# An identity matrix made on VectorE instead of GpSimd, and a first block's products in another order

## The chip, the cores and the metric

The kernel runs on one core of a Trainium2 chip. Its engines work side by side, each through its own list of instructions: TensorE (matrix products; PE in the profile, its weight loads PEld), VectorE (DVE), ScalarE (ACT), GpSimd (POOL) and SyncE (SP, which here only issues transfers). An engine waits on semaphores that others raise. Transfers (DMA) are issued from the queues of SP, ACT and POOL and run on 16 DMA engines. The metric is the device time of one execution in microseconds. It was 277.08 us before the change, the median of three runs (276.8 to 277.09).

## The reference

A dense layer, a GELU, a second dense layer, and the gradients of everything. Inputs are in bf16: x (1, 2048, 448), w1 (448, 1792), b1, w2 (1792, 448), b2 and grad_out, here g, in x's shape.

```python
def _gelu(x):
    return jax.nn.gelu(x, approximate=True)

def _fwd_reference(x, w1, b1, w2, b2):
    h = jnp.einsum("bsd,df->bsf", x, w1) + b1
    h = _gelu(h)
    return jnp.einsum("bsf,fd->bsd", h, w2) + b2

def reference(x, w1, b1, w2, b2, grad_out):
    _out, _vjp = jax.vjp(_f, x, w1, b1, w2, b2)
    _grads = _vjp(grad_out)
    return (_out0, *[jnp.asarray(_g) for _g in _grads])
```

So there are six outputs: the layer's output and the gradients of x, w1, b1, w2 and b2.

## The kernel before

All work is written in one order by hand; each engine takes its instructions in that order, and waits are put in where data or buffers ask for them. Hidden features lie on the partitions: a step g handles two tiles of 128 features (h = 0, 1) for one block of 512 rows. There are four blocks of seven steps, 28 steps in all. The first block begins with row 512, since `row0(b)` turns the blocks by one.

In a step, TensorE makes u = w1ᵀ xᵀ (`M1`, L243, and its last 64 of 448 rows in `rest`, L253) and q = w2 gᵀ (`M4`, L262, and `rest`, L256). ScalarE takes u out of PSUM with the bias (L288), squares it (L289), makes the GELU (L290) and a tanh (L382). VectorE builds the argument of the tanh (L379), the GELU's slope (L386 to L389) and multiplies it with q (`dve_gate`, L393). The two results, h and gh, are weights for the pieces of the output and of x's gradient (`Unit.piece`, L424). After the 28 steps come the last block's pieces, the gradient of w1 (L590, L598) and that of w2 (L609).

x, g and w2 come transposed by DMA on SP's queue (`load_x`, `load_g`, `load_w2T`), w1 and w2 plain; all early loads but three are issued from SP in one row, those three from ACT. g's first block is loaded in two halves of 256 rows.

The start differs from the other steps (step 0 is `first_products`, `turn_w2`, `first_chain`):
- VectorE clears four small tiles (L188 to L191). One is `warm`, which TensorE multiplies eight times (`keep_warm`, L282) before data is there.
- `make_identity`, a library helper (masks.py), makes a 128 x 128 identity in bf16, `ident`, in a part of the tile T that step 1 uses later: a memset on GpSimd (masks.py:197) and an affine select (masks.py:199).
- b1 comes as 14 rows of 128; VectorE turns it into a column for each tile with four 32 x 32 transposes (L484) and a cast (L485). The bias is first used by L325 on ScalarE and L326 on VectorE.
- `first_products` makes u of step 0, once for each half of the block's rows (L299, L302).
- `turn_w2` turns w2's first 256 rows on TensorE (the transposed loads bring the other rows): eight products of w2 (as weights) with `ident` (L313) into two PSUM tiles. `turned(0)` and `turned(1)` copy them to w2T on ScalarE (L317).
- `M1(1)` and `rest(1, None)` make u of step 1 (L243, L253).
- `first_chain` runs the GELU of step 0 in halves on ScalarE and VectorE, and then `first_q`: q of step 0 for each half r of g's rows, first with the row tiles 0 and 1 of g, then with 2 and the 64 rows that are left (L276). Between the two parts stand four products of the output (L424). `gate(0)` and `gate(1)` (L349) multiply the halves into gh.

Of the kernel before, what the change touches and what calls it, by code (L numbers as in the profile page):

```python
# [8 lines left out]

ACT = mybir.ActivationFunctionType  # L10
ALU = mybir.AluOpType
BF16 = mybir.dt.bfloat16
F32 = mybir.dt.float32
# [6 lines left out]
def kernel(  # L20
# [15 lines left out]
    nc = tc.nc  # L36
    P = 128
# [6 lines left out]
    KF = KD - 1  # L44
    DL = D - KF * P
    DOV = D - P
    DM = KF * P
    SB = 512
# [20 lines left out]
    psum_h = first.enter_context(tc.tile_pool(name="psum_h", bufs=1, space=bass.MemoryType.PSUM))  # L69
# [17 lines left out]
    T_flat = const.tile([P, 4 * 2 * SB], BF16, name="T")  # L87
# [5 lines left out]
    w2T_sb = w2T_flat.rearrange("p (k f) -> p k f", k=KD)  # L93
# [12 lines left out]
    def gq(b):  # L106
        o = ((b % 2) * 2 + 1) * KD * SB
        return xg_flat[:, o:o + KD * SB].rearrange("p (k s) -> p k s", k=KD)
# [5 lines left out]
    def hT(g):  # L114
        return ring(hT_flat, HR, g)

    def ghT(g):
        return ring(ghT_flat, GR, g)

    def V_of(g):  # L120
        return VA_flat[:, 0:2 * SB].rearrange("p (h s) -> p h s", h=2)

    def A_of(g):
        return VA_flat[:, 2 * SB:4 * SB].rearrange("p (h s) -> p h s", h=2)

    def B_of(g):
        return ring(B_flat, 1, g)

    def t_of(g):
        return ring(T_flat, 4, 2 * (g % 2))  # L130

    def p_of(g):
        return ring(T_flat, 4, 2 * (g % 2) + 1)
# [8 lines left out]
    HB = SB // 2  # L142
# [7 lines left out]
    def load_x(b, r0=0, r1=SB):  # L150
        src = x2[row0(b) + r0:row0(b) + r1, :]
        dst = xq(b)[:, :, r0:r1]
        if row0(b) > 0:
            turn_in(dst, src, DL - P)
        else:
            nc.sync.dma_start_transpose(out=dst[:, 0, :], in_=src[:, 0:P])
            nc.sync.dma_start_transpose(out=dst[:, 1:KD, :], in_=src[:, DL:D])
            nc.gpsimd.tensor_copy(out=dst[DL:P, 0, :], in_=dst[0:DL, 0, :])
# [30 lines left out]
    nc.vector.memset(ones, 1.0)  # L189
    nc.vector.memset(b1_rows, 0.0)  # L190
    nc.vector.memset(w128[:], 1.0 / P)  # L191
    ident = T_flat[:, 6 * SB:6 * SB + P]
    make_identity(nc, ident)
    load_x(0, 0, HB)
    load_x(0, HB, SB)
    nc.scalar.dma_start(out=w1_sb[:, 1:KD, 0:256], in_=w1[DL:D, 0:256].rearrange("(k p) f -> p k f", p=P))
# [28 lines left out]
    def blk(g):  # L225
        return divmod(g, NPAIR)

    def cols(g, h):
        c = g % NPAIR
        return slice((2 * c + h) * P, (2 * c + h + 1) * P)  # L230

    u_of = {}
    g_of = {}
# [28 lines left out]
                nc.tensor.matmul(g_of[g][:, h, :], lhsT=w2T_sb[:, kt, cols(g, h)], rhs=gq(g // NPAIR)[:, kt, :],  # L262
                                 start=False, stop=(kt == KF - 1), skip_group_check=True)

    def first_q(kts):


        for r in range(2):
            rs = slice(r * HB, (r + 1) * HB)
            if kts[0] == 0:  # L270
                g_of.setdefault(0, []).append(psum_h.tile([P, SB], F32, name="h%d" % r))
            q = g_of[0][r]
            for kt in kts:
                ps = slice(0, DL if kt == KF else P)
                for h in range(2):
                    nc.tensor.matmul(q[:, h * HB:(h + 1) * HB], lhsT=w2T_sb[ps, kt, cols(0, h)], rhs=gq(0)[ps, kt, rs],  # L276
                                     start=(kt == 0 and h == 0), stop=(kt == KF),
                                     tile_position=(0, 0) if kt == KF else None, skip_group_check=True)

    def keep_warm(n, weights, moving):  # L280
        for i in range(n):
# [34 lines left out]
    def turned(i):  # L316
        nc.scalar.copy(out=w2T_sb[:, 2 * i:2 * i + 2, 0:2 * P], in_=(ta, pw)[i].rearrange("p (k f) -> p k f", k=2))  # L317

    def first_chain():

        V, A, Bt, t, p, h0 = V_of(0), A_of(0), B_of(0), t_of(0), p_of(0), hT(0)
        R = (slice(0, HB), slice(HB, SB))

        def copy(r):
            nc.scalar.activation(out=V[:, 0, R[r]], in_=u_of[0][r][0], func=ACT.Identity, bias=b1_col[:, 0:1])  # L325
            nc.vector.tensor_scalar(out=V[:, 1, R[r]], in0=u_of[0][r][1], scalar1=b1_col[:, 1:2], scalar2=None,  # L326
                                    op0=ALU.add)

        def square(r):
            nc.scalar.activation(out=A[:, :, R[r]], in_=V[:, :, R[r]], func=ACT.Square,  # L330
                                 scale=math.sqrt(3.0 * GELU_C * GELU_A))

        def gelu(r):
            nc.scalar.activation(out=h0[:, :, R[r]], in_=V[:, :, R[r]], func=ACT.Gelu_apprx_tanh)

        def tanh(r):
            nc.scalar.activation(out=t[:, :, R[r]], in_=Bt[:, :, R[r]], func=ACT.Tanh, scale=-1.0 / 3.0)

        def cubic(r):
            nc.vector.scalar_tensor_tensor(out=Bt[:, :, R[r]], in0=A[:, :, R[r]], scalar=3.0 * GELU_C, in1=V[:, :, R[r]],  # L340
                                           op0=ALU.add, op1=ALU.mult)

        def slope(r):
            nc.vector.scalar_tensor_tensor(out=p[:, :, R[r]], in0=A[:, :, R[r]], scalar=GELU_C, in1=h0[:, :, R[r]],
                                           op0=ALU.add, op1=ALU.mult)
            nc.vector.tensor_scalar(out=p[:, :, R[r]], in0=p[:, :, R[r]], scalar1=-0.5, scalar2=None, op0=ALU.add)

        def gate(r):
            nc.vector.scalar_tensor_tensor(out=ghT(0)[:, :, R[r]], in0=t[:, :, R[r]], scalar=1.0,  # L349
                                           in1=g_of[0][r].rearrange("p (h s) -> p h s", h=2), op0=ALU.add, op1=ALU.mult)  # L350

        def times(r):
            nc.vector.tensor_scalar(out=t[:, :, R[r]], in0=t[:, :, R[r]], scalar1=1.0, scalar2=None, op0=ALU.add)
            nc.vector.tensor_tensor(out=t[:, :, R[r]], in0=t[:, :, R[r]], in1=p[:, :, R[r]], op=ALU.mult)

        copy(0)
        square(0)
        gelu(0)
        cubic(0)
        copy(1)  # L360
        turned(0)
        square(1)
        tanh(0)
        gelu(1)
        turned(1)
        slope(0)
        cubic(1)
        tanh(1)
        times(0)
        slope(1)  # L370
        times(1)
        first_q((0, 1))
        run_pieces([U["o", 0, j] for j in (0, 0, 1, 1)])
        first_q((2, KF))
        gate(0)
        gate(1)

# [70 lines left out]
    def run_pieces(units):  # L448
        for un in units:
            if un.piece():  # L450
                full.append(un)
# [7 lines left out]
    U = {(k, b, j): Unit(k, b, j) for k in "og" for b in range(NB) for j in range(SPB)}  # L459
# [28 lines left out]
    M1(1)  # L488
    rest(1, None)
    first_chain()  # L490
    first.close()
    psum_g = ctx.enter_context(tc.tile_pool(name="psum_g", bufs=1, space=bass.MemoryType.PSUM))
    for g in range(NSTEP):
        b, c = blk(g)
        pieces = [U[k] for k in seq[b] for _ in range(NF)]
        n = len(pieces)
# [84 lines left out]
    for t0, t1 in ((0, 4), (4, HT)):  # L581
        n = (t1 - t0) * P
        for h in range(2):
            a0, a1 = t0 + h * HT, t1 + h * HT
            cs = slice(a0 * P, a1 * P)
            for kt in range(KF):
                ps = psum_a.tile([P, SB], F32, name="acc")
                psv = ps[:, 0:n].rearrange("p (t f) -> p t f", f=P)
                for st in range(NS):
                    nc.tensor.matmul(psv, lhsT=x_all[:, st, kt * P:(kt + 1) * P], rhs=gh_rows(st, a0, a1),  # L590
                                     start=(st == 0), stop=(st == NS - 1))
                nc.scalar.copy(out=gw1_all[:, kt, cs], in_=ps[:, 0:n])  # L592
            nc.scalar.dma_start(out=out_2[0:KF * P, cs].rearrange("(k p) f -> p k f", p=P), in_=gw1_all[:, :, cs])
        ps = psum_a.tile([P, SB], F32, name="acc")
        for st in range(NS):
            for h in range(2):
                psv = ps[h * DL:(h + 1) * DL, 0:n].rearrange("p (t f) -> p t f", f=P)
                nc.tensor.matmul(psv, lhsT=x_all[:, st, KF * P:D], rhs=gh_rows(st, t0 + h * HT, t1 + h * HT),  # L598
                                 start=(st == 0), stop=(st == NS - 1), tile_position=(0, h * DL), skip_group_check=True)
        nc.scalar.copy(out=gw1_rem[:, t0 * P:t1 * P], in_=ps[:, 0:n])  # L600
        for h in range(2):
            nc.scalar.dma_start(out=out_2[KF * P:D, (t0 + h * HT) * P:(t1 + h * HT) * P],
                                in_=gw1_rem[h * DL:(h + 1) * DL, t0 * P:t1 * P])


    for ft in range(NF):
        ps = psum_a.tile([P, SB], F32, name="acc")
# [41 lines left out]
```

## Time and profile before

| | |
|---|---|
| time, median of three runs | 277.08 us |
| the profiled execution's own time | 276.89 us |
| its span, first to last instruction | 275.1 us |
| granted TensorE clock | 1.000 |
| TensorE busy | 266.6 us, 97% of the span |
| VectorE busy | 191.0 us, 69% |
| ScalarE busy | 145.2 us, 53% |
| GpSimd busy | 54.4 us, 20% |
| TensorE in the first 7.30 us / from 7.30 to 9.20 us | 5.81 / 0.06 us busy |
| VectorE from 14.8 to 40.0 us | 24.10 of 25.20 us busy |

The profile is of one execution. Times in it count from the first instruction. A line number stands for the source line that made an instruction; where a library made it, its file is named. Tiles are called by the names of the buffers they lie in: `w_x` holds w1, `w_gw` w2, `w2T_g` w2 transposed, `xg_h` the turned x and g, `T` several small tiles, `ident` among them. An instruction of a sequencer (a register move, a semaphore, a configuration, a DMA issue) is not counted as busy. "Landing" is the time from a DMA's issue to its last semaphore update.

### The profile page before, as it was taken

How to read it: one execution, taken by the hardware profiler on the slowest of the kernel's cores; microseconds unless marked ns; L12 is line 12 of the kernel's file. 1: busy time of each engine (PE TensorE's matmuls, PEld its weight loads, DVE VectorE, ACT ScalarE, POOL GpSimd, SP SyncE). 2: the span in 40 equal slices, each digit the busy share in tenths (PEclk: the TensorE clock that was granted, in tenths of full speed). 3: DMA queues.
4: the chain of work that ended last, by engine and by line, in shares of the span. 5: the costliest groups of instructions: out<-in, count | busy, mean ns of one | idle time of the engine just before them, and what ended most of it. 6: DMA issues, size and time to landing. Idle time of an engine off the chain costs nothing.

```text
span 275.1 us, 3612 instructions
## 1 busy us (share of the span) xinstructions
PE 266.6 (97%) x1397; PEld 124.8 (45%) x1411; DVE 191.0 (69%) x229; ACT 145.2 (53%) x193; POOL 54.4 (20%) x61
## 2 busy tenths in 40 slices
PE   7799999999999999999999999999999999999995
PEld 3343434344344434444444445554445655555552
DVE  2799999999999999999988871149999960000000
ACT  3787888788888878887677750021111211112111
POOL 0000000850211503032030236111700039200000
DMA  7999899999589956245634329999989931101111
GB/s 163 210 270 218 154 218 173 210 328 163 120 204 193 265 69 134 52 132 122 161 110 79 111 80 217 314 343 252 182 170 308 209 101 57 38 15 50 52 49 34
DMA packets 100477, 43.52 MB, mean 158 GB/s; under 512 B 89036, under 2 KB 97100, under 8 KB 100460
## 3 DMA queue, kind: packets, MB, share of 16 engines
q1 hardware_dynamic: 93376, 26.65, 51.0%
q0 software_dynamic: 4512, 14.69, 17.2%
q10 hardware_dynamic: 2572, 1.95, 2.3%
q8 instruction: 11, 0.18, 0.3%
q14 instruction: 6, 0.05, 0.1%
HBM read 7.00 MB, written 14.23 MB: 77 GB/s over the span
## 4 chain that ended last, share of the span: by engine, by line
PE 85%; DVE 9%; issue 4%; ACT 1%; POOL 0%; DVEq 0%; POOLq 0%
PE acc L424 28%; PE acc L609 15%; PE acc L590 13%; PE q L262 11%; PE u L243 10%; PE u L253 4%; PE acc L598 2%; DVE ghT_h L393 2%; DVE T L386 2%; DVE Bt L379 2%; DVE T L389 1%; PE h L276 1%; DVE T L387 1%; DVE T L388 1%; PE q L256 0%
## 5 line engine op out<-in xcount | busy, mean ns | idle before, releaser
L424 PE MATMUL acc<-w_gw,hT_h 128*128 128x448 bf16 x224 | 46.5, 352 | 0.0
L424 PE MATMUL acc<-w1T_gw,ghT_h 128*128 128x448 bf16 x224 | 45.1, 352 | 0.0
L288 ACT ACTIVATE VA<-u,b_col 128x512 f32<-128x512 f32 x54 | 34.0, 681 | 13.3 <-PE u L253 13.3
L262 PE MATMUL q<-xg_h,w2T_g 128*128 128x512 bf16 x161 | 39.4, 381 | 0.2 <-issue 0.2
L243 PE MATMUL u<-xg_h,w_x 128*128 128x512 bf16 x149 | 38.4, 379 | 1.2 <-ACT VA L288 0.6
L393 DVE SCALAR_TENSOR_TENSOR ghT_h<-T,q 128x1024 bf16<-128x1024 bf16 x27 | 33.0, 1221 | 8.3 <-PE q L262 6.6
L590 PE MATMUL acc<-gh_nat,w_x 128*128 128x512 bf16 (+1 forms) x192 | 36.7, 353 | 0.0
L382 ACT ACTIVATE T<-Bt 128x1024 bf16<-128x1024 f32 x27 | 28.5, 1057 | 14.0 <-DVE Bt L379 13.9
L386 DVE SCALAR_TENSOR_TENSOR T<-VA,hT_h 128x1024 bf16<-128x1024 f32 x27 | 32.9, 1219 | 0.0
L379 DVE SCALAR_TENSOR_TENSOR Bt<-VA 128x1024 f32<-128x1024 f32 x27 | 32.9, 1218 | 0.0
L424 PEld LDWEIGHTS <-hT_h 128*128 128x128 bf16 x224 | 21.8, 98 | 21.4 <-issue 0.2
L424 PEld LDWEIGHTS <-ghT_h 128*128 128x128 bf16 x224 | 21.9, 98 | 20.9
L575 DVE TENSOR_TENSOR VA<-VA,gh_nat 128x1792 f32<-128x1792 f32 x14 | 30.0, 2142 | 0.5
L289 ACT ACTIVATE VA<-VA 128x1024 f32<-128x1024 f32 x27 | 28.5, 1057 | 0.9
L290 ACT ACTIVATE hT_h<-VA 128x1024 bf16<-128x1024 f32 x27 | 28.1, 1040 | 0.0
L590 PEld LDWEIGHTS <-w_x 128*128 128x128 bf16 x192 | 18.7, 98 | 17.8 <-issue 0.4
L262 PEld LDWEIGHTS <-w2T_g 128*128 128x128 bf16 x162 | 13.6, 97 | 24.2 <-issue 11.4
L611 ACT CAST w_gw<-acc 128x448 bf16<-128x448 f32 x13 | 6.9, 533 | 32.6 <-PE acc L609 32.6
L243 PEld LDWEIGHTS <-w_x 128*128 128x128 bf16 x162 | 15.7, 98 | 18.4 <-issue 0.8
L592 ACT CAST w1T_gw<-acc 128x512 bf16<-128x512 f32 (+1 forms) x12 | 6.3, 533 | 30.1 <-PE acc L590 23.1
L397 POOL DMA_DIRECT2D hT_dram<-hT_h x28 | 20.3, 727 | 1.3 <-DMA out_dram<-io_o 1.2
L438 ACT CAST io_g<-acc 128x448 bf16<-128x448 f32 x16 | 8.3, 520 | 22.6 <-PE acc L424 22.6
(77 smaller groups left out, 243.0 us busy)
## 6 DMA issues: line engine op xcount, KB each, us to landing
hT_dram<-hT_h POOLq DMA_DIRECT2D x28, 256.0 KB, 3.9
out_dram<-io_o POOLq DMA_DIRECT2D x8, 224.0 KB, 4.0
out_dram<-io_g POOLq DMA_DIRECT2D x8, 224.0 KB, 3.2
w_x<-in_x_dram POOLq DMA_DIRECT2D x1, 1344.0 KB, 10.1
w2T_g<-in_grad_out_dram POOLq DMA_DIRECT2D x1, 1344.0 KB, 13.4
out_dram<-w_gw SPq DMA_DIRECT2D x4, 336.0 KB, 2.4
w_x<-in_w_dram SPq DMA_DIRECT2D x2, 384.0 KB, 4.6
out_dram<-w1T_gw ACTq DMA_DIRECT2D x2, 384.0 KB, 4.6
```

Of the source, the lines that this page charges most:

```text
L243: nc.tensor.matmul(u_of[g][h], lhsT=w1_sb[:, 1 + kt, cols(g, h)], rhs=xq(g // NPAIR)[:, 1 + kt, :], start=(kt == 0), stop=False, skip_grou ...
L262: nc.tensor.matmul(g_of[g][:, h, :], lhsT=w2T_sb[:, kt, cols(g, h)], rhs=gq(g // NPAIR)[:, kt, :], start=False, stop=(kt == KF - 1), skip_ ...
L288: nc.scalar.activation(out=V_of(g)[:, h, :], in_=u[h], func=ACT.Identity, bias=b1_col[:, ft:ft + 1])
L289: nc.scalar.activation(out=A_of(g), in_=V_of(g), func=ACT.Square, scale=math.sqrt(3.0 * GELU_C * GELU_A))
L379: nc.vector.scalar_tensor_tensor(out=B_of(g), in0=A_of(g), scalar=3.0 * GELU_C, in1=V_of(g), op0=ALU.add, op1=ALU.mult)
L382: nc.scalar.activation(out=t_of(g), in_=B_of(g), func=ACT.Tanh, scale=-1.0 / 3.0)
L386: nc.vector.scalar_tensor_tensor(out=p_of(g), in0=A_of(g), scalar=GELU_C, in1=hT(g), op0=ALU.add, op1=ALU.mult)
L393: nc.vector.scalar_tensor_tensor(out=ghT(g), in0=t_of(g), scalar=1.0, in1=q[:], op0=ALU.add, op1=ALU.mult)
L424: nc.tensor.matmul(self.ps[:, 0:D], lhsT=lhsT, rhs=rhs, start=(ft == 0), stop=(ft == NF - 1 and not bias))
L575: nc.vector.tensor_tensor(out=gsb_v, in0=gsb_v, in1=gh_rows(st, 0, NF), op=ALU.add)
L590: nc.tensor.matmul(psv, lhsT=x_all[:, st, kt * P:(kt + 1) * P], rhs=gh_rows(st, a0, a1), start=(st == 0), stop=(st == NS - 1))
L609: nc.tensor.matmul(ps[:, 0:D], lhsT=h_blk[ft][:, st, :], rhs=g_all[:, st, :], start=(st == 0), stop=(st == NS - 1))
```

## The change

The identity is now made by VectorE, in 13 instructions, right behind its four memsets and ahead of b1's transposes. A row `number` holds 0 to 127 on every partition: a memset of its first column, then seven adds, each of which doubles the length. Four 32 x 32 transposes turn parts of it into `row`, which holds a partition's own number in 32 columns. One compare of `number` with `row`, repeated four times, gives ones where they agree. `number` and `row` lie behind `ident` in the same tile. GpSimd's memset and select are gone.

`first_q` now makes one half of g's rows in a call. For each half come the parts of row tiles 0 and 1 and then two products of the output; the parts 2 and the rest follow for both halves as before. The order was: both halves' first parts, four products, both halves' last parts.

```diff
-from concourse.masks import make_identity
...
-    ident = T_flat[:, 6 * SB:6 * SB + P]
-    make_identity(nc, ident)
+
+    ident, number, row = (T_flat[:, 6 * SB + i * P:6 * SB + i * P + n] for i, n in enumerate((P, P, 32)))
+    nc.vector.memset(number[:, 0:1], 0.0)
+    for k in range(7):
+        nc.vector.tensor_scalar(out=number[:, 1 << k:2 << k], in0=number[:, 0:1 << k], scalar1=float(1 << k), scalar2=None,
+                                op0=ALU.add)
+    for i in range(P // 32):
+        nc.vector.transpose(out=row[32 * i:32 * (i + 1), :], in_=number[0:32, 32 * i:32 * (i + 1)])
+    nc.vector.tensor_tensor(out=ident.rearrange("p (a b) -> p a b", b=32), in0=number.rearrange("p (a b) -> p a b", b=32),
+                            in1=row[:, None, :].to_broadcast([P, P // 32, 32]), op=ALU.is_equal)
     load_x(0, 0, HB)
     load_x(0, HB, SB)
...
-    def first_q(kts):
-
-
-        for r in range(2):
-            rs = slice(r * HB, (r + 1) * HB)
...
+    def first_q(r, kts):
+
+
+        rs = slice(r * HB, (r + 1) * HB)
...
-        first_q((0, 1))
-        run_pieces([U["o", 0, j] for j in (0, 0, 1, 1)])
-        first_q((2, KF))
+        for r in range(2):
+            first_q(r, (0, 1))
+            run_pieces([U["o", 0, r]] * 2)
+        for r in range(2):
+            first_q(r, (2, KF))
         gate(0)
         gate(1)
```

More of the change, by code (lines that the diff above doesn't have):

```diff
@@ L263, in M4 @@
                                  start=False, stop=(kt == KF - 1), skip_group_check=True)
-    def first_q(kts):
-        for r in range(2):
-            rs = slice(r * HB, (r + 1) * HB)
[L270 to L278, printed above, removed]
+    def first_q(r, kts):
+        rs = slice(r * HB, (r + 1) * HB)
+        if kts[0] == 0:
+            g_of.setdefault(0, []).append(psum_h.tile([P, SB], F32, name="h%d" % r))
+        q = g_of[0][r]
+        for kt in kts:
+            ps = slice(0, DL if kt == KF else P)
+            for h in range(2):
+                nc.tensor.matmul(q[:, h * HB:(h + 1) * HB], lhsT=w2T_sb[ps, kt, cols(0, h)], rhs=gq(0)[ps, kt, rs],
+                                 start=(kt == 0 and h == 0), stop=(kt == KF),
+                                 tile_position=(0, 0) if kt == KF else None, skip_group_check=True)
     def keep_warm(n, weights, moving):
```

## The prediction

> **What bounds the kernel now.** I read the chain of waits first, over the whole span and then over its first 40 us, because the change touches only the start. It shows whether the start is on the path at all. Columns: start in us, length in us, what ran.
>
> ```profile
> 0.99 7.74 issue
> 8.73 0.36 POOL T masks.py:199
> 9.10 0.04 issue
> 9.14 0.72 PE acc L313 x8
> 9.87 1.40 PE u L243 x6
> 11.27 0.54 PE u L253 x2
> 11.80 0.98 PE h L276 x8
> ...
> 14.76 0.69 DVE ghT_h L349
> 15.45 0.53 DVE Bt L379
> ...
> 39.55 0.45 issue
> 40.00 1.23 DVE ghT_h L393
> 41.23 0.04 issue
> 41.27 0.37 PE q L256
> ```
>
> The chain that ends the kernel starts with the identity. GpSimd sits for 7.74 us with nothing that the profile shows, makes the identity (masks.py:199), and TensorE turns w2 with it (L313). From there on the chain has no slack: TensorE to 14.76, VectorE's run of the first block to 41.2, then TensorE almost without a break to the last product (ACT holds it once, near 49). So time taken from before 9.14 reaches the end, provided that nothing else comes last in its place. Next the timeline of the first 24 us, to see what that could be (start, length, engine, line, what; in brackets the idle time before it and what ended it).
>
> ```profile
> 4.26 0.85 DVE L484 STREAM_TRANSPOSE T<-T 32x32 bf16<-32x32 bf16 x4 [2.90 <-DMA T<-in_b_dram]
> 5.14 0.17 DVE L485 CAST b_col<-T 128x14 f32<-128x14 bf16 x1
> 5.90 0.47 ACT L325 ACTIVATE VA<-acc,b_col 128x256 f32<-128x256 f32 x1 [1.84 <-PE acc L302]
> 7.42 0.10 PEld L313 LDWEIGHTS <-w_gw 128*128 128x128 bf16 x1 [0.43 <-DMA w_gw<-in_w_dram]
> 7.64 0.45 ACT L325 ACTIVATE VA<-h,b_col 128x256 f32<-128x256 f32 x1
> 8.73 0.35 POOL masks.py:199 TENSOR_SCALAR_AFFINE_SELECT T<-T 128x128 bf16<-128x128 bf16 x1 [7.80 <-issue]
> 9.14 0.72 PE L313 MATMUL acc<-T,w_gw 128*128 128x128 bf16 x8 [1.87 <-POOL T masks.py:199]
> 9.56 0.59 ACT L317 CAST w2T_g<-acc 128x512 bf16<-128x512 f32 x1 [1.47 <-PE acc L313]
> ```
>
> TensorE ends its previous product at 7.27 and idles 1.87 us. The first weights of L313, rows of w2, are in at 7.42 to 7.52; only the identity is missing until 9.14. VectorE is idle from 1.36, the end of its memsets, to 4.26, when b1 lands.
>
> **What is removed.** On GpSimd a memset, a register move, two MODIFY_POOL_CONFIG (trace rows at 0.95 and 0.98) and the select. With them goes TensorE's wait. First product of L313 without it: weights loaded, 7.52, against 9.14, so 1.62 us. Bounds: w2's load was issued at 3.57 and took 3.8 us; the loads issued in the first 14 us took 2.6 to 4.8. At 2.6 TensorE itself is last (its end at 7.27; gain 1.8); at 4.8 w2 lands at 8.4 and the gain is 0.6. I take the measured 3.8.
>
> The row says why the select is late: the config pair stands right before it, the memset before that ran at 0.73, and nothing else fills 0.99 to 8.73. [...]
>
> **What is added.** Thirteen small VectorE instructions, each needing the one before, queued between the memsets (end 1.36) and b1's transposes (L484, L485), which L325 on ACT and L326 on VectorE wait for.
> - One memset of a column: 0.06 to 0.17 (rows L189, L191); 0.1.
> - Seven adds of 1 to 64 columns. bf16 TENSOR_SCALAR takes 0.29 at 512 columns (L346) and 0.42 at 1024 (L388), so about 0.16 of fixed cost, plus the 0.03 between dependent instructions (11.61 to 11.64): 7 x 0.19 = 1.33.
> - Four transposes: the same as L484's four, 0.85, plus 0.03.
> - One compare over 128 columns: TENSOR_TENSOR takes 0.43 at 512 (L354) and 0.69 at 1024 (L389), so 0.16 + 0.07, plus 0.03: 0.26.
>
> Sum 2.6 us: from 1.36 to 3.9. It lies wholly in the 2.90 us of idle before b1 lands, and the identity is there 3.5 us before w2. Cost on the path: 0. If that cover is too short: b1's column is ready at 5.31 and first needed at 5.90, so another 0.6 is free; beyond it ACT's chain is late. Bounds per instruction: 0.06 (L189) to 0.48 (L326, an f32 form); I take the bf16 rows, since the new tiles are bf16 and narrower than any of them. At 0.48 the sum is 6.2; that is a rival below.
>
> **What is moved.** first_q's first parts, with two products of the output between the two halves. The work is the same: 16 products of 256 columns, 4 of 448, no DMA, nothing past a queue of SP, ACT or POOL. What it costs: two more changes between the two kinds. L276 to L424 starts 0.11 later (12.51 to 12.62), L424 to L276 0.19 (13.18 to 13.37); these are the ordinary spacings, so 0; upper bound 0.1 each from the spacing at the 64-row parts (13.48 to 13.69, where 0.11 is usual). What it gains: g's second half is issued at 6.65 and lands 3.7 later, 10.37. First_q now starts at 11.73, after the shift at 10.11; in the old order its second half would start 0.44 later, 10.55, in the new one after two more products of 0.19, 10.93. The load is in either way: 0 gain, and 0.56 of room instead of 0.18.
>
> **What is late next.** All of this moves up by 1.62, so each load must be in by then. w1's next columns (issued 4.20, 3.8 to land: 7.95 to 8.0) are needed at 9.80 - 1.62 = 8.18: 0.2 of room, the tightest. Their last 64 rows (4.69 + 3.7 = 8.4) are needed at 9.57. g's first half (5.30 + 4.2 = 9.5) at 10.11. w2T's second columns (9.50 + 3.8 = 13.3) at 16.81 - 1.62 = 15.2, the next (12.53 + 4.7 = 17.2) at 19.9. All there. SP's queue issues these in a row and was waiting for none of the engines moved here, so it does not move. ACT: L317 was released by TensorE at 9.56 and becomes bound by L325's end, 8.00 (its starts overlap the one before by 0.1): 1.56 up. Gate 0 (L349) waits for TensorE by 0.45 now and by about 0.3 then, since VectorE follows ACT up by 1.5 to 1.56. A at L379 ends at 14.97 - 1.56 = 13.41, before gate 1 is through (15.45 - 1.62 = 13.83). So the whole chain moves 1.62.
>
> GpSimd's remaining early work, the copy L166 at 29.81 (0.40), is needed by L256 at 41.27. The two all-reduces (194.3 and 224.8, with their own config pair at 188.5) end 40 us before the kernel does. One item is unexplained: 0.45 of "issue" before the gate at 40.00. I leave it as it is; it may vanish or come twice, +-0.45.
>
> **Sum.** -1.62 + 0 + 0 = -1.62. The profiled execution took 276.89 (span 275.1 and 1.8 around it), so 275.27; the runs' median is 277.08, 0.19 above it, which gives 275.46. I say 275.4. A difference of 0.2% (0.55 us) is about what a measurement of this kernel can tell from no change.
>
> **Rivals.**
> - A load becomes last (the wait is only renamed). For it: 0.2 of room at w1's columns, and w2 itself sets 7.42. Against: both landings are measured. With w2 or w1 0.4 to 1.0 later: 275.9 to 276.5.
> [...]
> - VectorE is the slower maker (the other side). At 0.48 each the thirteen end at 7.6, b1's column at 8.7, ACT's first copy at 8.8 instead of 5.90. Then L317 starts at 10.9, 1.3 after its present 9.56; A has 0.39 of room at L379, so about 1.0 slower: 278.1. Break-even: L317 may come 0.39 after its present start, 9.95, so ACT's first copy at 7.85, so the thirteen end by 6.75: 5.4 us, 0.41 each, twice my 0.2. For it: unseen widths and partition-crossing transposes. Against: every bf16 row of this size.
> - The gain is eaten later (a stall at a fixed time in 15 to 41). For it: the unexplained 0.45 at 40.00. Against: no DMA wait in that stretch of the chain. Within 0.5 of before: 276.6 to 277.4.
>
> **Chances.** Forecast 0.80 (own range 274.9 to 275.8: -0.45 of the stall, +0.4 of the changes and room); load last 0.10; VectorE slower 0.03; code load exposed 0.01; eaten later 0.06. Faster by over 0.2% (below 276.5): 0.80 + 0.10 = 0.90. Within 0.2%: the eaten case, 0.06. Slower: 0.04. The range reaches from the forecast's low end through the load case, 274.9 to 276.4.
>
> **What would show it.** Right: no GpSimd instruction before L166; the compare done near 3.9, L484 still at 4.26; TensorE's idle before L313 0.2 to 0.3 and ended by w2's load; L313 at 7.5, L349's second part at 13.1, the gate now at 40.00 at about 38.4, the last product 1.6 earlier. Wrong: L484 after 4.9; a DMA named before L243 or L276; a second "issue" gap on VectorE before 40; L256 waiting for POOL.

## The result and the profile after

The changed kernel takes 274.83 us, the median of six runs (274.73 to 275.39), beside 276.88 for the kernel before (six runs, 276.61 to 277.09). The ratio is 0.9930, with a 95% interval of 0.9917 to 0.9943: faster by 2.05 us (0.7%), where 1.62 had been worked out. The 274.83 lies 0.07 below the low end of the stated range, 274.9; the kernel before is itself 0.2 lower in these six runs than in the three on which the forecast was built (276.88, 277.08), and as a share of that kernel's time the result lies inside the range. The profiled execution took 274.79; its span is 273.0 us, 2.1 less than before.

The chain of waits of the changed kernel, over its first 45 us (start, length, what ran):

```profile
0.73 4.16 DMA xg_h<-in_x_dram
4.93 0.82 PE acc L305 x6
5.76 0.32 PE acc L308 x2
6.08 0.32 PE acc L288
6.40 0.66 PE h L305 x6
7.06 0.32 PE h L308 x2
7.38 0.67 PE acc L319 x8
...
12.97 0.69 DVE ghT_h L355
13.65 1.13 DVE Bt L387
```

GpSimd is gone from it. The chain now begins with x's first transfer, and TensorE runs from x's landing through step 0's products straight into turning w2 (L319, L313 before). The second gate of step 0 (L355) begins at 12.97 instead of 14.76. From the timeline of the same execution (start, length, engine, line, what; in brackets the idle time before it and what ended it):

```profile
1.32 0.06 DVE L193 MEMSET T<- 128x1 bf16 x1
1.41 1.40 DVE L195 TENSOR_SCALAR T<-T 128x1 bf16<-128x1 bf16 x7
2.72 0.84 DVE L198 STREAM_TRANSPOSE T<-T 32x32 bf16<-32x32 bf16 x4
3.60 0.23 DVE L199 TENSOR_TENSOR T<-T 128x128 bf16<-128x128 bf16 x1
3.88 0.85 DVE L492 STREAM_TRANSPOSE T<-T 32x32 bf16<-32x32 bf16 x4
7.31 0.58 PEld L319 LDWEIGHTS <-w_gw 128*128 128x128 bf16 x8 [0.21 <-DMA w_gw<-in_w_dram]
7.31 0.74 PE L319 MATMUL acc<-T,w_gw 128*128 128x128 bf16 x8
8.11 0.57 ACT L323 CAST w2T_g<-acc 128x512 bf16<-128x512 f32 x1
```

VectorE's identity stands at 3.82, 3.5 us before TensorE wants it. TensorE's row at L319 has no bracket: it does not idle there. Nor does it at L250, but only just: w1's second columns landed at 7.96, and L250 uses them from 8.00. L319 starts 1.83 us earlier than its forerunner (9.14). The gates show how that travels: the step-1 gate moves from 19.30 to 17.50 (1.80), the one of step 5 from 40.00 to 37.91 (2.09), the last from 162.59 to 160.49 (2.10). So 1.8 us come from the wait, and some 0.3 more appear between the two steps, where neither kernel has changed instructions.

### The profile page after: what moved, and what is told of

It reads as the page before. It is cut to its first block, busy times and chain, and to the rows that moved or that the text cites. A ratio compares the mean times of both kernels' runs of the same rounds, so it can differ in the third digit from the quotient of the medians.

```text
span 273.0 us, 3631 instructions
## 1 busy us (share of the span) xinstructions
PE 267.8 (98%) x1411; PEld 124.9 (46%) x1411; DVE 193.1 (71%) x242; ACT 145.0 (53%) x193; POOL 54.2 (20%) x59
## 4 chain that ended last, share of the span: by engine, by line
PE 84%; DVE 12%; DMA 2%; ACT 0%; issue 0%; DVEq 0%
PE acc L432 27%; PE acc L617 16%; PE acc L598 13%; PE q L269 10%; PE u L250 10%; PE u L260 4%; DVE T L394 3%; DVE Bt L387 3%; DVE ghT_h L401 3%; PE acc L606 2%; DVE T L397 2%; DMA xg_h<-in_x_dram 2%; DVE T L395 1%; PE h L282 1%; DVE T L396 1%; PE acc L305 0%
## 5 line engine op out<-in xcount | busy, mean ns | idle before, releaser
L250 PE MATMUL u<-xg_h,w_x 128*128 128x512 bf16 x162 | 39.4, 379 | 0.6 <-ACT VA L294 0.6
L390 ACT ACTIVATE T<-Bt 128x1024 bf16<-128x1024 f32 x27 | 28.5, 1057 | 13.2 <-DVE Bt L387 13.1
L250 PEld LDWEIGHTS <-w_x 128*128 128x128 bf16 x162 | 15.8, 98 | 18.4 <-issue 0.8
```

The source lines that it names most:

```text
L250: nc.tensor.matmul(u_of[g][h], lhsT=w1_sb[:, 1 + kt, cols(g, h)], rhs=xq(g // NPAIR)[:, 1 + kt, :], start=(kt == 0), stop=False, skip_grou ...
L390: nc.scalar.activation(out=t_of(g), in_=B_of(g), func=ACT.Tanh, scale=-1.0 / 3.0)
```

## Experiments: which part, and why GpSimd was late

The theory is that TensorE's wait for the identity was all of it, that the order is worth nothing, and that what made GpSimd late was the config pair of its select, with no harm to anything else. Rivals: the order carries a part; what GpSimd does behind that pair, in 7.74 us of which no row shows anything, slows others; whatever comes first on GpSimd is late. Each group below ran on one chip of its own, beside the kernel before: 276.92 in this one.

**The identity alone**, first_q in the old order:

```diff
-        for r in range(2):
-            first_q(r, (0, 1))
-            run_pieces([U["o", 0, r]] * 2)
+        first_q(0, (0, 1))
+        first_q(1, (0, 1))
+        run_pieces([U["o", 0, j] for j in (0, 0, 1, 1)])
```

> The identity by VectorE as in the changed kernel, first_q in the old order. Theory A (the wait for the identity is the whole of it, the order is worth nothing): as the changed kernel, 274.8, within 0.2. Theory B (the new order carries a part): g's second half landed at 10.48 in the changed kernel's trace and would be needed at 10.45 in the old order, so TensorE idles there by up to 0.1, or by 0.4 if the load slips: 274.9 to 275.3.

Measured: 275.48 (275.19 to 275.65), ratio 0.9941 (0.9919 to 0.9962).

**The order alone**, the identity by GpSimd:

```diff
+    ident = T_flat[:, 6 * SB:6 * SB + P]
+    make_identity(nc, ident)
-    ident, number, row = ...
```

> The identity by GpSimd as before, first_q in the new order. Theory A: as the kernel before, 276.9, within 0.2, since g's second half is there 1.8 us before its use. Theory B (the order itself is worth something, or costs through more changes between products of different kinds): 276.5, or 277.1.

Measured: 276.79, ratio 0.9994 (0.9972 to 1.0017). The order alone makes no difference that shows. The identity alone, at 275.48, lies above 274.8 and would by itself fit a share of the order. But two kernels of this group with the new order (275.31 and 275.32, below) stand only 0.17 from it, and its ratio lies amid the three that the changed kernel gave in three groups (0.9930, 0.9942, 0.9951). If the order is worth anything, it is too little to show. In the profile of the identity alone g's second half landed at 10.47 and was first used at 11.37, so nothing waited for it. Where w2 is turned 1.0 us earlier, as in the first profile of the changed kernel, the old order would want it near 10.4, about when it lands (10.48 there): by this estimate some 0.1 us, which no run here tells from nothing.

**A select that nobody waits for**, beside the changed kernel:

```diff
+    make_identity(nc, T_flat[:, 7 * SB:7 * SB + P])
```

> The changed kernel, and beside it GpSimd makes an identity (memset, config pair, select) in columns that nobody reads. Theory A (what cost was TensorE's wait for it): GpSimd's select ends near 9.1 again, L319 and its heirs start near 7.3 all the same, 274.8 within 0.2. [...]

Measured: 275.31, ratio 0.9937 (0.9916 to 0.9959). The timeline, GpSimd and TensorE:

```profile
0.73 0.20 POOL masks.py:197 MEMSET T<- 128x128 bf16 x1 [0.29 <-POOLq L643]
8.56 0.28 POOL masks.py:199 TENSOR_SCALAR_AFFINE_SELECT T<-T 128x128 bf16<-128x128 bf16 x1 [7.63 <-issue]
...
7.96 0.74 PE L321 MATMUL acc<-T,w_gw 128*128 128x128 bf16 x8
```

The select is as late as before (8.56, and 8.73 before), and TensorE does not wait for it. The time lies 0.3 above what theory A allowed, but the kernels of this group that have no select at all take as much (275.48 above, 275.32 below), and what made L321 late in this profile was TensorE's first six products, 1.44 us instead of 0.82; w2, at 7.54, was in before. The gain stays, within the intervals: the wait cost, not the select beside it.

**GpSimd back in the path with a copy** in place of the select:

```diff
-    nc.vector.tensor_tensor(out=ident.rearrange(...), ...)
+    made = T_flat[:, 7 * SB:7 * SB + P]
+    nc.vector.tensor_tensor(out=made.rearrange(...), ...)
+    nc.gpsimd.tensor_copy(out=ident, in_=made)
```

> The changed kernel, but VectorE's compare goes to other columns and GpSimd copies them into the identity: GpSimd is in the path again, with a copy instead of a select. [...] Theory D (whatever comes first on GpSimd after its memsets is some 8 us late): the copy runs near 8 to 9, 276.5 to 276.9.

Measured: 275.32, ratio 0.9944 (0.9916 to 0.9973). The copy in the timeline:

```profile
3.89 0.29 POOL L202 COPY T<-T 128x128 bf16<-128x128 bf16 x1 [3.45 <-DVE T L200]
```

It runs 0.07 after VectorE's compare ends, where theory D had it near 8 to 9. The time itself, 0.3 above the range of theory A (274.8 within 0.2), is that of its group. So GpSimd as an engine is prompt here; only the select, behind its MODIFY_POOL_CONFIG pair, came 7.4 to 8.0 us after what stood before it (four profiles with it: 7.74, 7.95, 7.57, 7.43 us from the pair's end to the select). Pair and select always came together, so no run tells which of them costs the time.

A second pair, late in the program, says a little more. It stands ahead of the first all-reduce. In the four profiles with a select that all-reduce began 5.7 to 7.1 us behind its pair, 1.4 to 3.0 us after the last semaphore row of GpSimd ahead of it (194.31 in the kernel before, behind a pair that ends at 188.57 and a semaphore row that ends at 192.42). In the ten without a select it began 0.01 us after that row (192.08 to 192.09 in the changed kernel), as little as 3.7 us behind its pair. So where a select had run, GpSimd lost time at the next pair too, and a pair alone does not always cost 7 us. None of this was on the path: the all-reduces end 40 us before the kernel does.

## Experiments: the 0.3 us that the sum did not have, and what is last now

**The changed kernel again**, on another chip (before: 277.06), as a measure:

> The changed kernel itself, beside the other runs. Theory A (order and GpSimd's beside-work are worth nothing, and the four runs before it differ from 274.8 only by how early TensorE's clock came up and x landed): 275.2 to 275.5 here too, beside 276.9 for the kernel before. Theory B (the new order carries 0.2 to 0.6): 274.8 here, while the old order gave 275.5.

Measured: 275.06, ratio 0.9942 (0.9919 to 0.9964), 2.00 faster than before: between the figures of the two theories, so it does not part them. Its profiled execution was not typical; it took 277.22, and its chain says why:

```profile
5.14 1.44 PE acc L305 x6
6.58 0.54 PE acc L308 x2
7.12 0.54 PE acc L288
7.66 1.28 PE h L305 x6
8.94 0.54 PE h L308 x2
9.48 1.10 PE acc L319 x8
10.58 1.45 PE u L250 x6
```

The same products as in the chain above, at about half the rate: 1.44 and 1.28 for what took 0.82 and 0.66, 1.10 for 0.67. Only L250 runs at the usual rate. TensorE reaches L319 at 9.41, 2.1 us later than in the first profile, and the whole gain is gone in this execution. In the identity-alone profile the first six products were slow too (1.44), the second six not (0.65).

**The kernel before, with VectorE's instruction numbers shifted** by 13 tiny memsets:

```diff
     make_identity(nc, ident)
+    for i in range(13):
+        nc.vector.memset(T_flat[0:1, 7 * SB + 2 * i:7 * SB + 2 * i + 1], 0.0)
```

> The kernel before, with 13 more one-element memsets on VectorE behind its first four (some 0.8 us of its 2.9 idle us), so that its later instructions have the numbers that they have in the changed kernel. Theory E (VectorE's stop of 0.45 us ahead of the gate at 40.0 comes at a certain instruction number): no stop at 40.0, a stop of 0.0 to 0.2 near 29 to 34 instead, 276.5 to 276.7. Theory F (the stop comes from what runs at that time): it stays at 40.0, 276.9.

Measured: 276.34, 0.72 below the kernel before, ratio 0.9978 (0.9960 to 0.9996). The stop of 0.45 ahead of the gate at 40.0 is not there; the timeline has one longer row instead, some ten us earlier (the other rows of this kind take 1.22):

```profile
30.42 1.37 DVE L381 SCALAR_TENSOR_TENSOR Bt<-VA 128x1024 f32<-128x1024 f32 x1
31.71 1.21 DVE L388 SCALAR_TENSOR_TENSOR T<-VA,hT_h 128x1024 bf16<-128x1024 f32 x1
```

The changed kernel has the same, by 0.20, at nearly the same place:

```profile
29.92 1.42 DVE L394 SCALAR_TENSOR_TENSOR T<-VA,hT_h 128x1024 bf16<-128x1024 f32 x1
31.26 0.41 DVE L395 TENSOR_SCALAR T<-T 128x1024 bf16<-128x1024 bf16 x1
```

Counted with its semaphore rows, the longer row is VectorE's 64th in the padded kernel and its 63rd in the changed one, and the gate at 40.0 is the 64th in the kernel before. Theory E stands, though the time is below the 276.5 to 276.7 that it gave. Of the 0.72 the profile explains 0.27 by the stop (the gate is 0.43 earlier, L313 only 0.16 earlier); the interval reaches down to 0.1, so how much of the rest is real stays open.

**b1 late**, by a memset and 14 adds behind the identity:

```diff
+    extra = T_flat[:, 7 * SB:7 * SB + 64]
+    nc.vector.memset(extra, 0.0)
+    for i in range(14):
+        nc.vector.tensor_scalar(out=extra, in0=extra, scalar1=1.0, scalar2=None, op0=ALU.add)
     load_x(0, 0, HB)
```

> The changed kernel, with a memset and 14 dependent adds of 64 columns on VectorE between the identity and b1's transposes: 3.0 us more, some 5.4 in all for the identity and these, which the prediction gave as the break-even with the kernel before (so 276.9). From the changed kernel's trace: b1's column at 4.94 + 3.0 = 7.95 instead of needed by 6.01, so ACT's chain is 1.9 late with less than 0.1 of room at the first gate: 1.8 of the gain are gone, 276.6 to 277.1. If VectorE's queue had cover to spare there: 274.8 to 275.5.

Measured: 276.51 (276.48 to 276.69), ratio 0.9981 (0.9971 to 0.9992): 1.45 of the 2.00 gone, 0.1 short of the lower of the times expected. The timeline, VectorE and ScalarE:

```profile
3.89 3.00 DVE L204 TENSOR_SCALAR T<-T 128x64 bf16<-128x64 bf16 x14
6.80 0.84 DVE L496 STREAM_TRANSPOSE T<-T 32x32 bf16<-32x32 bf16 x4
...
7.95 0.47 ACT L335 ACTIVATE VA<-acc,b_col 128x256 f32<-128x256 f32 x1 [3.90 <-PE h L312]
...
9.96 0.57 ACT L327 CAST w2T_g<-acc 128x512 bf16<-128x512 f32 x1
```

VectorE's added work ends at 6.89 (1.36 to 6.89 is 5.5 us), ScalarE copies at 7.95 and again at 9.96. The step-1 gate begins at 19.31, against 19.30 in the kernel before. That is the break-even, where the prediction put it. Of the 0.55 that are left, 0.4 are the stop before 40.0 (the gate there begins at 39.60), which this kernel's profile does not show.

**Without the filler product** between the halves of step 0's products:

```diff
-            if r == 0:
-                keep_warm(1, warm[:, 0:P], warm)
```

> The changed kernel without the one product of cleared data between the two halves of step 0's products (0.32 us in the chain of the changed kernel; in the kernel before it lay ahead of TensorE's wait). Theory G (TensorE's own work from x's landing on is now the path): 0.1 to 0.4 faster than the changed kernel, with w2 (7.1 to 7.5) or w1's second columns (7.95 to 8.4) last then. Theory H (a load was last already): no change.

Measured: 275.37, ratio 0.9947 (0.9929 to 0.9965), against 0.9942 for the changed kernel: no gain. Its chain:

```profile
4.80 1.29 PE acc L305 x6
6.09 0.34 PE acc L308 x2
6.46 0.49 DVE VA L330
7.03 0.63 ACT VA L334
7.66 0.52 ACT hT_h L338
8.18 0.36 ACT VA L329
8.54 0.29 ACT w2T_g L321
```

TensorE is ahead by the product, and the chain goes over VectorE and ScalarE instead, up to the copy of w2T. Neither theory had named that: ScalarE's copies are right behind TensorE. A load is as near: w1's second columns landed at 8.09 in this profile, and TensorE used them from 8.14.

In a last group (before: 276.82) the changed kernel ran a third time, with three variants.

> The changed kernel once more, as the measure for the three beside it: 274.8 to 275.2; 277 where TensorE's clock comes up only after 9 us.

Measured: 275.56 (275.07 to 275.64), ratio 0.9951 (0.9939 to 0.9964): 1.26 faster, and 0.4 slower than expected. Its profiled execution is the fastest of the five (275.07, full rate from x's landing on), so what the usual ones lost is not shown.

**Ten filler products** ahead of x instead of eight (`keep_warm(10, ...)`):

> The changed kernel with ten products of cleared data ahead of x instead of eight, so that TensorE has no idle time between them and x's landing (4.6 to 4.9 or 5.4). Theory I (that idle time delays the clock's rise): no first products at half rate (0.22 us a product of 256 columns), 0.0 to 0.4 faster than the changed kernel. Theory J (the rise comes at a time of its own that varies from execution to execution): products at half rate in some executions all the same, and TensorE starts x's products up to 0.5 later: 0.1 to 0.4 slower.

Measured: 275.62, ratio 0.9957 (0.9944 to 0.9969). The first six products took 1.25 us, 0.21 apart, although TensorE had no idle time before them. Theory I falls, by this one profile; the 0.1 to 0.4 of theory J lies within the noise.

**w2's load one place later** on SP's queue:

```diff
-    load_w2(0, 2)
     load_w1(nc.sync, 256, 512)
+    load_w2(0, 2)
```

> The changed kernel with w2's first load behind w1's second columns on SP's queue instead of ahead of them: w2 lands 1.0 to 1.1 later, 8.1 to 8.5, and TensorE, ready at 7.4 to 8.0, waits for it. By the prediction's rival (a load becomes last) 0.3 to 1.0 of the gain are gone: 275.3 to 276.0. If the load had room: no change.

Measured: 275.66, ratio 0.9958 (0.9946 to 0.9971), no change. The load was issued at 4.75 instead of 3.52 but took 3.0 us instead of 3.6, and landed at 7.74, with TensorE's turning of w2 at 7.78. The landing expected at 8.1 to 8.5 did not come: the transfer's time is not fixed, and the delay was too small to tell the price.

**The stop moved into idle time**: 40 one-element memsets behind b1's cast in the changed kernel:

```diff
     nc.vector.tensor_copy(out=b1_col[:], in_=b1_turned[:, 0:NF])
+    for i in range(40):
+        nc.vector.memset(T_flat[0:1, 7 * SB + 2 * i:7 * SB + 2 * i + 1], 0.0)
```

> The changed kernel with 40 one-element memsets on VectorE behind b1's cast (0.01 apart in the trace of the padded kernel before, so about 0.5 us of the 1.1 that VectorE idles there). By theory E the stop at VectorE's 63rd or 64th instruction falls into that idle time: none from 15 to 45, 0.0 to 0.2 faster than the changed kernel. By theory F: as the changed kernel, with its stop of 0.2 near 30.

Measured: 275.39, ratio 0.9952 (0.9938 to 0.9965), no measurable gain over the 275.56 beside it. But its timeline shows two things, first on VectorE, then on TensorE:

```profile
5.17 0.63 DVE L495 MEMSET T<- 1x1 bf16 x39
6.19 0.06 DVE L495 MEMSET T<- 1x1 bf16 x1 [0.39 <-issue]
...
9.32 1.47 PE L250 MATMUL u<-xg_h,w_x 128*128 128x512 bf16 x6 [0.58 <-DMA w_x<-in_w_dram]
```

The stop has come along to VectorE's 64th row, now a memset, so here it goes by the count of instructions and not by what runs at the time. And in this execution (276.04) w1's second columns landed at 9.28, 5.1 us after their issue, and TensorE waited 0.58 us for them: the prediction's first rival, seen in one execution, though not in the typical one.

## Why the prediction was right

One relation holds the profiles together. Take each profiled execution's time, and subtract the start of turning w2:

| kernel | time | w2 turned from | difference |
|---|---|---|---|
| before | 276.89 | 9.14 | 267.75 |
| order alone | 277.35 | 9.59 | 267.76 |
| before, padded | 276.47 | 8.98 | 267.49 |
| changed | 274.79 | 7.31 | 267.48 |
| identity alone | 275.65 | 8.32 | 267.33 |
| changed, dead select | 275.46 | 7.96 | 267.50 |
| changed, GpSimd copy | 275.32 | 7.77 | 267.55 |
| changed, third group | 275.07 | 7.57 | 267.50 |
| changed, ten fillers | 275.92 | 8.43 | 267.49 |

From that product on nothing but VectorE's stop differs: 267.75 with the stop of 0.45, 267.3 to 267.6 with a smaller one or none. Left out are the four profiles in which something else came last behind that product: b1 (268.64), ScalarE's copies without the filler (267.72), w1's columns (268.03) and the slow products of the 277.22 execution (267.81); the one with w2's load later has 267.45.

- **The wait removed.** Worked out as 1.62, bounds 0.6 and 1.8. The step held, and its size was 1.83 in the first pair of profiles: w2 landed at 7.10 instead of 7.38, which left TensorE itself last, the case given the upper bound. In the other profiles of kernels without the wait L319's start lies between 7.43 and 8.43, 0.7 to 1.7 ahead of 9.14, apart from the slow one at 9.41.
- **VectorE's thirteen instructions.** 2.6 us ending at 3.9; measured 2.5, ending at 3.82, term by term 0.06, 1.40, 0.84 and 0.23. They were hidden, as said. b1's transposes began at 3.88 and not "still at 4.26": the cover was narrower than the row of before let it seem, since b1 was in earlier. The room behind it was not touched: b1's column was ready at 4.94 and first used at 6.01.
- **The order.** 0, and the runs show no difference.
- **What moves behind it.** L323 at 8.11 (predicted 8.00), the second part of L355 at 12.97 (13.1): the path through TensorE and ScalarE moved as worked out. Behind the four constants that it writes by 0.45, GpSimd has no instruction before its copy of w2T's end, at 29.00 now. The copy took 1.26 us instead of 0.40, but came without a delay like the 7.74 us ahead of the select, and nothing waited for it.
- **The stop at 40.0.** "It may vanish or come twice, +-0.45", and it was taken as unchanged. It shrank to 0.20 and moved. The first sum was short by 0.43, and this term is the larger part of it: some 0.25 here and 0.21 in the wait above. The gate was expected at 38.4 and came at 37.91.
- **What the prediction did not name.** It took TensorE's readiness at 7.27 as fixed. That time depends on x's landing (4.8 to 5.4) and on when TensorE's clock comes up (4.65 to 6.81, once 10.64), and both were hidden behind 1.87 us of waiting. With the wait gone they show: the gain is 2.05, 2.00 and 1.26 in three groups. That these lie on both sides of 1.62 is partly chance. The load rival had the right consequence, a smaller gain, but w1's columns were clearly last in one profile only; in the others x's landing and TensorE's slow start set the time.
- **The delay on GpSimd.** The 7.74 us ahead of the select, on which the prediction built, came again as 7.43 to 7.95 in the three other profiles with a select, and the gain came. The chances give 0.01 to a code load exposed; no run shows a code load. What the runs show is these 7.43 to 7.95 us without a row, behind the config pair, and in the changed kernel a copy at 29.00 for which nothing waited.
- **The slower maker.** The break-even of 5.4 us was tested and met to 0.1 us in the step-1 gate.

## What to carry to other kernels

Before costing a removed wait, ask what else was hidden behind it, the clock's rise (4.65 to 6.81 us here, once 10.64) and the spread of transfers (x landed at 4.8 to 5.4) as well as the next data: the gain ends where the next of these comes last, and it varies when they do. GpSimd's affine select at the start of the program, with the config pair ahead of it, came near 9 us here and was a poor thing to have on the path, while VectorE could build the same constant in 2.5 us of time in which it had nothing to do. A stall that the profile calls "issue" and that no wait explains should be looked up by the instruction's number on its engine: padding moved it.

## What the runs showed of the hardware that was not expected

**TensorE's rate at the start varies from execution to execution, and the profile's windows hide it.** The products of 256 columns in step 0 start 0.11 us apart at full rate and 0.21 to 0.22 at half. With the first product at 1.18 before and after the change, the full rate was there by 4.93 in the first profile of the changed kernel, between 6.3 and 7.2 in the identity-alone one, and only after 10 us in the execution of 277.22. All windows show a clock of 1.00 there, but only because a stretch for which the trace holds no record of the clock reads 1.00. Twelve of the fourteen traces hold such records, and in them the full clock begins at 4.65 to 6.81 us in eleven (4.99 in the first profile of the changed kernel, where it lasts 269.65) and at 10.64 in the execution of 277.22, where the spacing of the products changes too. So TensorE's rise to the full rate varies by 2.2 us over eleven profiles and by 6.0 with the twelfth, with no cause in the kernel that these runs found. Why that one rose so late stays open.

**VectorE stops once near its 63rd to 65th recorded instruction** (semaphore rows counted), for 0.45 us in the kernel before and the one with the order alone, 0.39 in the padded changed one, 0.15 to 0.2 in eight other profiles, and not visibly in three. Transfers of 8192 bytes on the queue that the profile calls instruction stand in the trace near several of them (29.33 in the changed kernel, with its longer row at 29.92). In the three with the longest stops the nearest one comes behind the stop (40.91 in the kernel before, 41.40 with the order alone, 8.08 in the padded changed kernel). No run shows what causes the stop.
